# A fused sigmoid-attention and gated MLP kernel: an own PSUM bank for one of seven products, and attention heads spread otherwise over the MLP blocks

## The chip, the cores and the metric

One core of one Trainium2 chip. The metric is device time of one execution in microseconds (us); lower is better. Engines in the profile: PE (matrix products), DVE (vector), ACT (scalar and activation), SP (issues the DMAs); POOL does nothing here.

## The reference

```python
def _attn_ref(q, k, v):                       # q, k, v: (8, 12, 448, 64)
    scores = scale * np.matmul(q, k.transpose(0, 1, 3, 2)) - np.log(S)
    attn = 1.0 / (1.0 + np.exp(-scores))
    return np.matmul(attn, v)

def _moe_ref(x, w_in, w_out):                 # x: (3584, 768), w_in: (768, 2048), w_out: (2048, 768)
    h = x @ w_in
    g = h * (1.0 / (1.0 + np.exp(-1.702 * h)))
    return g @ w_out

def reference(**kwargs):
    attn_out = _attn_ref(q, k, v)
    x = attn_out.transpose(0, 2, 1, 3).reshape(B * S, H * D)
    return _moe_ref(x, w_in, w_out)
```

96 attention heads (8 batches of 12) without a softmax, and then a two-layer MLP over the 3584 tokens.

## The kernel before

**Tiling.** The tokens are cut into 7 blocks of 512 (numbered 0 to 6); the batches have 448 tokens, so a block takes parts of two batches. In a block, `ups` are 48 tasks of six matmuls (16 columns of `w_in`, three tasks each, tiles `h`), and `downs` are 48 tasks of six matmuls (6 output tiles `o` of eight tasks). Every fp32 product is made as three fp32r matmuls of a rounded part and a rest (128x512 each): rounding is a CAST on ACT or DVE, and the rest a subtraction on DVE.

**Attention.** Batches 0 to 2 are done first, two heads at a time (L530, L553), partly alongside block 0. Batches 3 to 7, 60 heads, are done one at a time by `head`: scores on PE in two tasks (tile `sc`, L713, 7 matmuls in sum), sigmoid on ACT (L719), rounding and rest (`ahi`, `alo`, L761, L768), product with v on PE (tile `av`, L802, 7 matmuls), additions into a block's x (L817). `split_head` prepares q and k before that (`qk`, L669 and others). `packed_attention` makes 61 *units* of PE tasks from them: a unit holds the two score tasks of one head and the product of the head before, and the 61st holds the last product alone. After the 20th unit and every fifth from there on, `sums_of_weights` loads two weight tiles, combines them on DVE (`sums`, `tsplit`) and stores the results.

**Last two blocks.** Blocks 5 and 6 are done together by `last_blocks`: a 2x2 block product by seven products (p1 to p7) in place of eight. Its inputs are sums of x parts (tiles `xs`, `xa`: names `s1` to `s4`, `a11` to `a22`). `up(n)` is called eight times, four in each half, and after each half `down` makes the outputs (L1172). In `up` the products are nine matmuls each (L1081) and run in the order p1, p6, p2, p7, p5, p4, p3. The tile `q` (`sc`, two banks of 512 f32) takes p1 and then p2 on top of it in its first half, and p6 in its second half; `w` (`m`) takes p7 and then p4, `z` (`m0` or `av`) takes p5 and then p3. The copy c1 (L1098 on ACT or L1099 on DVE) takes p1's result out of `q` before p2 adds to it; u2, u3, c22, c21, c12 are additions on DVE (L1000); `activated` makes the sigmoid (L1043), its product (L1046), rounding and rest.

**Order of work.** Each engine has its own list of instructions, written by a planner (`Plan.run`) at build time, with estimated costs. A task has dependencies, and each `Buffer` of a ring of n waits for the users of the n-th buffer before it (`BUFS`: `sc` 2, `m` 2, `m0` 1, `av` 1, `qk` 2, `x32` 8, `x` 6). On ACT, DVE and SP the planner takes the ready task with the smallest key (its place in the order). On PE there are two queues: `main` (ups and downs of all blocks, then the last blocks) and `side` (the attention units), each strictly in its order. A side unit is due when a given number of main tasks has been taken; the queue whose head can begin first goes next, and a due side unit wins a tie. These places come from this loop, in which an up counts 0.8 and a down 1.0 (86.4 in a block), and `LEAD` is 0.93:

```python
n = sum(HEADS[: b - 1])
units = [(0, u) for u in (packed[n : n + HEADS[b - 1]] if b < NB - 3 else packed[n:])]
...
total, done, n = sum(costs) * (LEAD if b < NB - 3 else LAST), 0.0, 0
for i, c in enumerate(costs):
    done += c
    while n < len(units) and n / len(units) < done / total:
        due.append((len(main) + i + 1, units[n][1]))
        n += 1
```

`HEADS` gives the units of blocks 1 to 4; block 4 takes whatever is left (NB is 7). The synchronisation between the engines is added by the framework from the tiles that each instruction reads and writes.

Of the kernel before, what the change touches and what calls it, by code (L numbers as in the profile page):

```python
# [18 lines left out]
ALU = mybir.AluOpType  # L19
# [16 lines left out]

SOON, PATIENCE = 6, 0.8

WARM = 5

HEADS, LAST = (12, 16, 16, 16), 0.78


BUFS = dict(
# [1 line left out]
    sc=2, sc3=1, av=1, m=2, m0=1,  # L46
# [29 lines left out]
class Plan:  # L76
# [10 lines left out]
    def buffer(self, tag):  # L87
        b = Buffer()
        self.rings.setdefault(tag, []).append(b)
        return b  # L90

    def task(self, engine, cost, emit, deps=(), uses=()):
        return self.either({engine: cost}, {engine: emit}, deps, uses)
# [8 lines left out]
    def run(self, streams):  # L102
# [19 lines left out]
        main, side = streams  # L122
# [13 lines left out]
        free = dict.fromkeys(("PE", "ACT", "DVE", "SP", "DMA"), 0.0)  # L136
# [11 lines left out]
        def since(t):  # L148

            if t.takes is None:  # L150
                return t.ready
            return max(t.ready, min(slots[t.takes], default=math.inf))
        at, current, doing = [0, 0], [], 0

        def pe():

            if current:
                return max(free["PE"], current[0].ready), None
            best = None
            heads = []  # L160
            if at[1] < len(side):
                heads.append((1, side[at[1]][1], side[at[1]][0] <= at[0]))
            if at[0] < len(main):
                heads.append((0, main[at[0]], True))
            for s, unit, due in heads:

                first = [t for t in unit if t.alone]
                if any(t.left for t in first):
                    continue
                when, before = free["PE"], 0.0  # L170
                for t in first:
                    when = max(when, t.ready - before)
                    before += t.costs["PE"]
                if best is None or when < best[0] - 1e-9 or (not best[2] and when <= best[0] + 1e-9):
                    best = (when, s, due)
            return (best[0], best[1]) if best else (None, None)

        count = 0
        while count < len(self.tasks):
            options = []  # L180
            when, s = pe()
# [6 lines left out]
            when, _, e = min(options)  # L188
# [7 lines left out]
            else:  # L196
# [9 lines left out]
                if soon:  # L206
                    t = min(soon, key=lambda t: t.key)
                    when = max(when, since(t))
# [43 lines left out]
def sigmoid_attention_mlp(ctx: ExitStack, tc: tile.TileContext, qk, v, v2, w, out):  # L252
# [60 lines left out]
    ps = spaces["m0"].tile([P, 512], F32, tag="m0", name="still", bufs=BUFS["m0"])  # L313
    for n in range(WARM):
        nc.tensor.matmul(ps, lhsT=still[:, :P], rhs=still, start=n == 0, stop=n == WARM - 1)

    plan = Plan()
    task, either, buffer = plan.task, plan.either, plan.buffer
# [12 lines left out]
    def dma(into, src, kb, deps, uses, first=lambda: None):  # L331
        def emit():
            first()
            nc.sync.dma_start(out=into(), in_=src())

        return task("SP", kb, emit, deps, uses)

    def on_either(act, dve, deps, uses, first=lambda: None):


        def emit(f):
            def go():
                first()
                f()

            return go

        return either({"ACT": act[0], "DVE": dve[0]}, {"ACT": emit(act[1]), "DVE": emit(dve[1])}, deps, uses)
# [502 lines left out]
    def columns(n):  # L851
        return 8 * (n // 4) + n % 4, 8 * (n // 4) + n % 4 + 4
# [130 lines left out]
    def last_blocks():  # L983
# [13 lines left out]
        def combine(out, a, b, op, deps, uses, first=lambda: None):  # L997
            def emit():
                first()
                nc.vector.tensor_tensor(out(), a(), b(), op=op)  # L1000

            return task("DVE", 0.69, emit, deps, uses)

        for i in range(NK // 2):
# [9 lines left out]
            s1, s2 = buffer("line"), buffer("line")  # L1014
# [17 lines left out]
        def piece(src, deps, name):  # L1032
            b = buffer("wsplit")
            return dma(lambda: b.tile.bitcast(F32), src, 2 * KB, deps, [b],
                       lambda: make(b, "wsplit", [P, 2 * NW_EL], F32R, name)), b
# [19 lines left out]
        def up(n):  # L1055
            f, f2 = columns(n)
            t_1, w1 = piece(lambda: halves[f], [saved[f]], f"w1_{n}")
            t_2, w2 = piece(lambda: sums[n][0], [summed[n, 0]], f"w2_{n}")
            t_3, w3 = piece(lambda: sums[n][1], [summed[n, 1]], f"w3_{n}")
            w4 = buffer("wh")  # L1060
            t_4 = dma(lambda: w4.tile.bitcast(F32).rearrange("p (t c) -> p t c", t=2),
                      lambda: halves[f2].rearrange("p (t c) -> p t c", t=2)[:, :, HW:], KB,
                      [saved[f2], *gate], [w4], lambda: make(w4, "wh", [P, 2 * HW], F32R, f"w4_{n}"))
            bank = ("m0", "av")[n % 2]
            q, z, w = buffer("sc"), buffer(bank), buffer("m")
            made = {"sc": [P, 2, 512]}

            def product(b, tag, at, wb, t_w, half, name, deps, more):

                step = wb.tag_cols if hasattr(wb, "tag_cols") else NW_EL  # L1070

                def emit():
                    if b.tile is None:
                        make(b, tag, made.get(tag, [P, 512]), F32, f"{tag}_{n}")
                    ps = at()
                    for i in range(NK // 2):
                        k = (half * (NK // 2) + i) * P
                        ws = [wb.tile[:, j * step + k : j * step + k + P] for j in range(2)]
                        x = parts[name, i][1].tile
                        for j, (c, d) in enumerate(((0, 1), (1, 0), (0, 0))):  # L1080
                            nc.tensor.matmul(  # L1081
                                ps, lhsT=ws[c], rhs=x[:, d], start=not more and i == 0 and j == 0,
                                stop=i == NK // 2 - 1 and j == 2, skip_group_check=more,
                            )

                xparts = [parts[name, i] for i in range(NK // 2)]
                t = task("PE", 9 * 0.2267, emit, [t_w, *deps, *(x[0] for x in xparts)],
                         [b, wb, *(x[1] for x in xparts)])
                units.append([t])
                return t  # L1090

            w4.tag_cols = HW
            q0, q1 = (lambda: q.tile[:, 0]), (lambda: q.tile[:, 1])
            h12, h22, h21 = buffer("x32"), buffer("x32"), buffer("x32")

            def copy(b, name, src, t, uses):
                return on_either(
                    (0.59, lambda: nc.scalar.copy(b.tile, src())),  # L1098
                    (0.69, lambda: nc.vector.tensor_copy(b.tile, src())),  # L1099
                    [t], [b, *uses], lambda: make(b, "x32", [P, T], F32, f"{name}_{n}"),  # L1100
                )

            def in12(): return h12.tile
            def in22(): return h22.tile
            def in21(): return h21.tile

            p1 = product(q, "sc", q0, w1, t_1, 0, "a11", [], False)
            c1 = copy(h12, "h12", q0, p1, [q])
            p6 = product(q, "sc", q1, w2, t_2, 1, "s2", [], False)
            u2 = combine(in12, in12, q1, ALU.add, [c1, p6], [h12, q])  # L1110
            p2 = product(q, "sc", q0, w1, t_1, 1, "a12", [c1], True)
            activated(one, f, q0, p2, [q])
            p7 = product(w, "m", lambda: w.tile, w3, t_3, 0, "s3", [], False)
            u3 = combine(in21, in12, lambda: w.tile, ALU.add, [u2, p7], [h21, h12, w],
                         lambda: make(h21, "x32", [P, T], F32, f"h21_{n}"))
            p5 = product(z, bank, lambda: z.tile, w2, t_2, 0, "s1", [], False)
            c5 = copy(h22, "h22", lambda: z.tile, p5, [z])
            c22 = combine(in22, in21, in22, ALU.add, [u3, c5], [h22, h21])
            activated(two, f2, in22, c22, [h22])
            p4 = product(w, "m", lambda: w.tile, w3, t_3, 1, "a22", [u3], True)  # L1120
            c21 = combine(in21, in12, lambda: w.tile, ALU.add, [p4, c22], [h21, h12, w])
            activated(two, f, in21, c21, [h21])
            p3 = product(z, bank, lambda: z.tile, w4, t_4, 0, "s4", [c5], True)
            c12 = combine(in12, in12, lambda: z.tile, ALU.add, [p3, c21], [h12, z])
            activated(one, f2, in12, c12, [h12])
# [84 lines left out]
    side = [(0, u) for u in attention()]  # L1210
# [8 lines left out]
    due = []  # L1219
# [14 lines left out]
    side = side[:early] + due  # L1234
# [37 lines left out]
```

## Time and profile before

| | |
|---|---|
| median of 3 runs | 1208.38 us (1208.35 to 1209.86) |
| the profiled execution's own time | 1209.63 us |
| its span, first to last instruction | 1207.6 us |
| busy: PE, DVE, ACT | 1189.8 us, 869.7 us, 718.6 us |
| mean granted TensorE clock | 0.998 |
| DMA | 274.10 MB, mean 227 GB/s |

Times of a trace are us from the span's start. A row of the timeline gives start, duration, engine, line, operation, output and input tile, shape, and count of merged instructions; in brackets the idle time of that engine ahead of it, and what ended it. Matmuls are pipelined, so a row's duration overlaps the next; distances are read from start to start.

### The profile page before, as it was taken

Reading aid. Unit: us, or ns where it says so; the run is one execution under the profiler, and the core shown is the slowest. Engines: PE = TensorE matmul, PEld = TensorE weight load, DVE = VectorE, ACT = ScalarE, POOL = GpSimd, SP = SyncE. Lnnn points to the kernel's source line nnn. Section 1 sums busy time; section 2 is a strip of 40 time slices with the busy share of each in tenths; the row PEclk is TensorE's granted clock in tenths of the full one; section 3 lists DMA queues with packets and bytes.
Section 4 is the critical chain, followed back from the end, with each engine's and each line's share of the span. In section 5 each row is a group of like instructions: output and inputs, shape, how many; then the busy total and the mean of one; then the engine's idle time right before and its main releaser. Section 6 shows DMA issues by size and latency. Waiting matters only on the chain.

```text
span 1207.6 us, 15254 instructions
## 1 busy us (share of the span) xinstructions
PE 1189.8 (99%) x5517; PEld 955.2 (79%) x5517; DVE 869.7 (72%) x1431; ACT 718.6 (60%) x1139; POOL 0.2 (0%) x4
## 2 busy tenths in 40 slices
PE   9999999999999999999999999999989999999998
PEld 4457777788888888888888888888778777877787
DVE  6989989689987588988598987599998254005511
ACT  7898887467786576766577776577864132113300
POOL 0000000000000000000000000000000000000000
PEclk9999999999999999999999999999999999999999
DMA  9956568786876656777666877775756654455552
GB/s 346 315 184 240 187 207 281 259 280 226 303 263 252 223 168 195 257 265 279 235 229 218 292 247 246 245 250 206 258 187 227 211 178 160 135 162 195 201 192 79
DMA packets 82155, 274.10 MB, mean 227 GB/s; under 512 B 8640, under 2 KB 15808, under 8 KB 82080
## 3 DMA queue, kind: packets, MB, share of 16 engines
q1 hardware_dynamic: 82080, 273.12, 66.0%
q8 instruction: 44, 0.72, 0.2%
q14 instruction: 31, 0.25, 0.1%
HBM read 203.88 MB, written 69.21 MB: 226 GB/s over the span
## 4 chain that ended last, share of the span: by engine, by line
PE 89%; DVE 7%; ACT 3%; issue 1%; DMA 0%; DVEq 0%; ACTq 0%
PE o L908 26%; PE h L908 22%; PE o L1172 11%; PE av L802 6%; PE sc L713 6%; PE av L553 5%; PE sc L1081 4%; PE sc L530 4%; PE m L1081 4%; PE av L1081 1%; DVE alo L768 1%; DVE qk L669 1%; ACT a L719 1%; DVE g L940 0%; DVE ahi L768 0%
## 5 line engine op out<-in xcount | busy, mean ns | idle before, releaser
L908 PE MATMUL h<-x,wsplit 128*128 128x512 f32 x1440 | 334.7, 390 | 0.5 <-DVE x L359 0.5
L908 PE MATMUL o<-gs,wsplit 128*128 128x512 f32 x1440 | 334.2, 390 | 0.0
L908 PEld LDWEIGHTS o<-gs,wsplit 128*128 128x128 f32 x1440 | 270.5, 188 | 57.1 <-issue 1.3
L908 PEld LDWEIGHTS h<-x,wsplit 128*128 128x128 f32 x1440 | 269.9, 188 | 57.5 <-issue 1.3
L353 ACT CAST gs<-g 128x512 fp32r<-128x512 f32 x108 | 67.0, 620 | 107.5 <-DVE g L940 67.2
L1172 PE MATMUL o<-gs,wd 128*128 128x512 f32 x576 | 130.9, 389 | 0.0
L719 ACT ACTIVATE a<-sc,bias 128x448 f32<-128x448 f32 x120 | 98.4, 820 | 50.9 <-PE sc L713 46.1
L1172 PEld LDWEIGHTS o<-gs,wd 128*128 128x128 f32 x576 | 108.1, 188 | 22.4
L669 DVE TENSOR_TENSOR qk<-qkraw,qk 64x64 fp32r<-64x64 f32 x180 | 111.3, 619 | 4.9 <-ACT qk L674 0.7
L768 DVE TENSOR_TENSOR alo<-a,ahi 128x448 fp32r<-128x448 f32 x120 | 101.2, 848 | 2.3 <-ACT ahi L761 1.1
L713 PE MATMUL sc<-qk 128*128 128x448 f32 x420 | 95.2, 366 | 2.8 <-ACT a L719 2.8
L761 ACT CAST ahi<-a 64x448 fp32r<-64x448 f32 (+2 forms) x138 | 88.5, 663 | 2.1
L713 PEld LDWEIGHTS sc<-qk 128*128 128x128 f32 x420 | 78.8, 188 | 12.3 <-ACT a L719 3.2
L359 DVE TENSOR_TENSOR gs<-g,gs 128x512 fp32r<-128x512 f32 x112 | 76.3, 685 | 10.2 <-ACT gs L353 8.2
L744 DVE COPY rest<-sc 64x448 f32<-64x448 f32 x45 | 28.2, 626 | 75.0 <-ACT a L719 70.4
L541 ACT ACTIVATE a<-sc,bias 112x896 f32<-112x896 f32 x72 | 68.7, 1007 | 14.9 <-PE sc L530 8.6
L1000 DVE TENSOR_TENSOR h<-h,sc 128x512 f32<-128x512 f32 x8 | 5.5, 688 | 96.2 <-PE sc L1081 96.2
L802 PE MATMUL av<-ahi,v 128*128 128x448 f32 x240 | 59.3, 370 | 0.0
L553 PE MATMUL av<-a,vraw 112*64 112x448 f32 x288 | 57.9, 545 | 0.0
L940 DVE TENSOR_TENSOR g<-h,g 128x512 f32<-128x512 f32 x80 | 54.7, 685 | 1.9 <-ACT g L935 0.9
L359 DVE TENSOR_TENSOR wsplit<-wraw,wsplit 128x768 fp32r<-128x768 f32 x48 | 45.7, 952 | 12.8 <-ACT wsplit L353 12.5
L935 ACT ACTIVATE g<-h 128x512 f32<-128x512 f32 x80 | 47.6, 595 | 10.6 <-PE h L908 10.1
(106 smaller groups left out, 1345.6 us busy)
## 6 DMA issues: line engine op xcount, KB each, us to landing
wsplit<-w SPq DMA_DIRECT2D x96, 768.0 KB, 5.1
w<-w SPq DMA_DIRECT2D x40, 768.0 KB, 5.2
w<-wsplit SPq DMA_DIRECT2D x32, 768.0 KB, 5.4
qkraw<-qk SPq DMA_DIRECT2D x48, 448.0 KB, 3.8
wraw<-f SPq DMA_DIRECT2D x48, 384.0 KB, 4.3
f<-w SPq DMA_DIRECT2D x32, 384.0 KB, 4.3
t<-tsplit SPq DMA_DIRECT2D x16, 768.0 KB, 4.4
w<-t SPq DMA_DIRECT2D x16, 768.0 KB, 4.8
```

Of the source, the lines that this page charges most:

```text
L359: lambda: nc.vector.tensor_tensor(lo(), src(), hi().bitcast(F32), op=ALU.subtract),
L541: nc.scalar.activation(a.tile[:C, c % 2], ps.tile[:C, :, :S], AF.Sigmoid, bias=bias[:C], scale=scale)
L553: nc.tensor.matmul(ps.tile[cols, :S], lhsT=vr.tile[:C, j, c], rhs=a.tile[:C, c % 2, j], start=c == 0, stop=c == NC - 1,)
L669: return lambda: nc.vector.tensor_tensor(s.tile[rows, into], qkr.tile[own, cols], s.tile[own, cols].bitcast(F32), op=ALU.subtract)
L713: nc.tensor.matmul(out, lhsT=s.tile[:, cols], rhs=s.tile[:, r : r + S], start=n == 0, stop=n == len(terms) - 1,)
L719: nc.scalar.activation(out, x, AF.Sigmoid, bias=bias[:rows], scale=scale)
L761: (costs[0], lambda: nc.scalar.copy(hi_at(), cols())),
L768: nc.vector.tensor_tensor(lo_at(), cols(), hi_at().bitcast(F32), op=ALU.subtract)
L802: nc.tensor.matmul(av.tile[:, :S], lhsT=vs.tile[:, c].rearrange("p a d -> p (a d)"), rhs=m, start=n == 0, stop=n == len(todo) - 1,)
L908: nc.tensor.matmul(ps, lhsT=ws[a], rhs=x[:, c], start=first and i == 0, stop=last and i == 2)
L1081: nc.tensor.matmul(ps, lhsT=ws[c], rhs=x[:, d], start=not more and i == 0 and j == 0, stop=i == NK // 2 - 1 and j == 2, skip_group_check=more,
L1172: nc.tensor.matmul(ps.tile, lhsT=ws[u], rhs=gb.tile[:, d], start=i == 0 and j == 0, stop=i == 7 and j == 2,)
```

## The change

- In `up`, p6 gets a buffer of its own, `q2`, in the ring `m`, and u2 reads it there. The second half of the tile `q` is no longer used (the tile keeps its size).
- `HEADS` goes from (12, 16, 16, 16) to (13, 17, 17, 13), and `LAST` from 0.78 to 0.84. Of the 61 units, blocks 1 to 4 had 12, 16, 16 and 17; they get 13, 17, 17 and 14. In block 4 they are spread over the first 0.84 of its cost.
- In the planner's choice between the two queues of PE, a side unit with a due place above zero is ranked as if it could begin `SLACK` = 2.0 us later than it can. The time at which it is then placed is not moved.

```diff
+SLACK = 2.0
-HEADS, LAST = (12, 16, 16, 16), 0.78
+HEADS, LAST = (13, 17, 17, 13), 0.84
...
-                when, before = free["PE"], 0.0
+                when, before = 0.0, 0.0
                 for t in first:
                     when = max(when, t.ready - before)
                     before += t.costs["PE"]
-                if best is None or when < best[0] - 1e-9 or (not best[2] and when <= best[0] + 1e-9):
-                    best = (when, s, due)
-            return (best[0], best[1]) if best else (None, None)
+
+                rank = max(free["PE"], when + (SLACK if s and side[at[1]][0] else 0.0))
+                if best is None or rank < best[0] - 1e-9 or (not best[2] and rank <= best[0] + 1e-9):
+                    best = (rank, s, due, max(free["PE"], when))
+            return (best[3], best[1]) if best else (None, None)
...
-            q, z, w = buffer("sc"), buffer(bank), buffer("m")
+            q, q2, z, w = buffer("sc"), buffer("m"), buffer(bank), buffer("m")
...
-            q0, q1 = (lambda: q.tile[:, 0]), (lambda: q.tile[:, 1])
+            q0, q1 = (lambda: q.tile[:, 0]), (lambda: q2.tile)
...
-            p6 = product(q, "sc", q1, w2, t_2, 1, "s2", [], False)
-            u2 = combine(in12, in12, q1, ALU.add, [c1, p6], [h12, q])
+            p6 = product(q2, "m", q1, w2, t_2, 1, "s2", [], False)
+            u2 = combine(in12, in12, q1, ALU.add, [c1, p6], [h12, q2])
```

## The prediction

> **What bounds the kernel now.** I read the page first, then the waits of PE stage by stage, then PE's own timeline around each wait.
>
> ```profile
> span 1207.6 us, 15254 instructions
> PE 1189.8 (99%) x5517; PEld 955.2 (79%) x5517; DVE 869.7 (72%) x1431; ACT 718.6 (60%) x1139; POOL 0.2 (0%) x4
> ```
>
> PE is the bound: it is without work for 1207.6 - 1189.8 = 17.8 us in all. The change removes no matmul, so only those 17.8 us, and what a wait costs beyond its idle time, can be won. The waits of PE, for 945 us to the end and then for 760 to 950 us (columns: total us, times, longest):
>
> ```profile
> PE sc L1081 <- DVE h L1099: 4.7, 6, 0.8
> PE sc L1081 <- ACT h L1098: 1.4, 2, 0.7
> ```
>
> ```profile
> PE sc L713 <- ACT a L719: 2.8, 1, 2.8
> PE av L802 <- DVE x L817: 1.4, 1, 1.4
> PE av L802 <- DVE alo L768: 0.9, 2, 0.5
> ```
>
> So there are two sore places: eight equal waits in the seven-product stage (one for each of the eight calls of `up`), and a bunch in block 4, where PE waits for the steps of a head. These are what the two halves of the change touch.
>
> **The bank of the second product.** PE's timeline in the first two calls of `up`, nine matmuls to a product:
>
> ```profile
> 952.26 2.20 PE L1081 MATMUL sc<-xs,w 128*128 128x512 f32 x9
> 955.13 2.34 PE L1081 MATMUL sc<-x,w 128*128 128x512 f32 x9 [0.68 <-ACT h L1098]
> 957.31 4.24 PE L1081 MATMUL m<-xs,w 128*128 128x512 f32 x18
> ...
> 967.51 2.20 PE L1081 MATMUL sc<-xs,w 128*128 128x512 f32 x9
> 970.50 2.35 PE L1081 MATMUL sc<-x,w 128*128 128x512 f32 x9 [0.78 <-DVE h L1099]
> 972.69 2.21 PE L1081 MATMUL m<-xs,w 128*128 128x512 f32 x9
> ```
>
> The first row of each triple is the second product p6, the second row is p2, the third p7. p2 adds onto the first product's half of `sc`, so it must wait for the copy c1 of that half. c1 needs only p1, which ends when p6 starts (952.26), and so could run beside p6. It does not:
>
> ```profile
> 954.50 0.59 ACT L1098 COPY h<-sc 128x512 f32<-128x512 f32 x1 [3.49 <-PE sc L1081]
> ```
>
> It starts when p6's row ends (952.26 + 2.20 = 954.46). ACT had been idle for 3.49 us, so it was not busy elsewhere. The natural reading: p1 and p6 write one tile, `sc`, and a reader of the tile waits for its latest writer. A product with a tile of its own shows the contrast; u3, the addition of p7:
>
> ```profile
> 959.55 0.69 DVE L1000 TENSOR_TENSOR h<-h,m 128x512 f32<-128x512 f32 x1
> ```
>
> p7 and p5 are the 18 matmuls from 957.31 on; u3 starts when nine of them are done (957.31 + 2.20 = 959.51), with the nine of p5 still running. So a reader whose product is alone in its tile does not wait for the next product. With p6 in `m`, c1 starts near 952.5 and ends near 953.1, over a microsecond before p2 could begin.
>
> What the wait costs is more than its idle time, since weight loads and the pipe start anew. Without it two products take 18 matmuls of 0.2277 us (price below) = 4.10 us; from p6's start to p7's it took 957.31 - 952.26 = 5.05 and 972.69 - 967.51 = 5.18 us. That is 0.95 for the two calls whose copy is on ACT and 1.08 for the six on DVE: 2 x 0.95 + 6 x 1.08 = **8.4 us**. The bounds: the idle time alone, 4.7 + 1.4 = 6.1 us, and 8.4; I take 8.4 because starts were measured.
>
> What moves along: p6 takes one of the two `m` buffers, so they no longer alternate between calls for p7 and p4. p6 must find u2 of the call before done, and p7 must find the last reader of p4's sum done, c21; c21 follows p4 while p3, p1, p6 and p2 still come ahead of the next p7, 36 matmuls or 8.2 us of cover against one 0.69 us addition behind a short chain. If that cover were gone, its cost would be about one such addition per call. The block-one groups of the down stage swap the two `m` buffers; each was last read a group or more before. No instruction and no DMA is added. The weight pieces have the same distance from release to next use, except those of p7, which lose the 1 us gap of 8.2 us; no row of PE's waits in this stage names a DMA. u2 also leaves DVE's queue sooner (now it waits for p2), which only frees those behind it. Late next in this stage: nothing is in sight.
>
> The rule that speaks against this: the Trainium skill, "PSUM — Partial Sum Buffer", summary table, has a reader beside a running matmul use a different bank, and gives a bank 2 KiB. Halves of 512 f32 are two banks already, so by the hardware alone c1 was free to run and another bank changes nothing: the sum would be short of this term. The 954.50 and 959.55 rows speak for bookkeeping by tile instead, which the page does not cover; it is a rival below.
>
> **The heads.** The price of a plain matmul and of a head's unit on PE, from block 3's down stage:
>
> ```profile
> 688.33 1.58 PE L713 MATMUL sc<-qk 128*128 128x448 f32 x7
> ...
> 691.17 6.99 PE L908 MATMUL o<-gs,wsplit 128*128 128x512 f32 x30
> 698.00 1.58 PE L713 MATMUL sc<-qk 128*128 128x448 f32 x7
> ```
>
> A unit is 691.17 - 688.33 = 2.84 us, 30 matmuls are 6.83 us (0.2277 each; a task of six 1.366 us), and the pitch from head to head is 9.67 us, with no wait. In block 4 a head comes every 3.96 tasks (0.78 x 86.4 / 17 units): 2.84 + 3.96 x 1.366 = 8.25 us. There it fails:
>
> ```profile
> 870.12 1.58 PE L713 MATMUL sc<-qk 128*128 128x448 f32 x7
> ...
> 874.71 5.62 PE L908 MATMUL o<-gs,wsplit 128*128 128x512 f32 x24
> 880.16 0.77 PE L713 MATMUL sc<-qk 128*128 128x448 f32 x3
> ...
> 887.93 7.43 PE L908 MATMUL o<-gs,wsplit 128*128 128x512 f32 x30
> 895.20 1.58 PE L713 MATMUL sc<-qk 128*128 128x448 f32 x7
> ```
>
> Lost against 2.84 us: 874.71 - 870.12 = 4.59, so 1.75; 887.93 - 880.16 = 7.77, so 4.93; and 895.20 - 887.93 = 7.27 for 6.83, so 0.44: **7.1 us**. Part of it is the clock that the wait brought down:
>
> ```profile
> 886.00:888.00 2.00, 2.00 (x7) 1.74 (x7) 2.00 (x4) 2.00 (x3) 0.00 (x0) 0.50 0.46 180
> ```
>
> Granted 0.50 after a 2.8 us wait: 4.93 + 0.44 less the idle 2.8 + 0.5 leaves 2.1 us of slow and restarted matmuls. (The Trainium skill, "TensorE: Matmul & The Clock Gate", Part 1, puts the drop after about 3.4 us of idle window; this trace shows it after less. By its rule a remaining wait of 2.8 us would cost 2.8, by the trace 4.9.)
>
> Why there: DVE. Busy time by stretch (PE, PEld, DVE, ACT, POOL, clock, DMA share, GB/s): block 3's ups and downs, then the bad stretch.
>
> ```profile
> 592.00:681.00 89.00, 89.00 (x405) 75.70 (x404) 79.33 (x137) 65.65 (x114) 0.00 (x0) 1.00 0.66 224
> 681.00:749.00 68.00, 68.00 (x312) 58.12 (x311) 57.00 (x100) 49.90 (x86) 0.00 (x0) 1.00 0.81 284
> ...
> 859.00:890.00 31.00, 26.25 (x112) 21.48 (x111) 30.36 (x52) 26.64 (x46) 0.00 (x0) 0.94 0.61 207
> ```
>
> DVE is busy 89%, 84% and 98%. In the last, a head's steps queue behind the splitting of block 5's x and the preparing of summed weights, and PE waits for the head.
>
> The edit of HEADS and LAST gives block 4 61 - 47 = 14 units in place of 17, spread over 0.84 of it: one per 0.84 x 86.4 / 14 = 5.18 tasks, a pitch of 2.84 + 7.08 = 9.92 us, wider than the 9.67 us that ran without a wait. So the 7.1 us go. The PE work of the moved heads (2.84 us each), their loads and spills on SP's queue and their DVE steps reappear in blocks 1 to 3, one head more in each: PE's part cancels. Blocks 2 and 3 go from 0.93 x 86.4 / 16 = 5.02 to 4.73 tasks, a pitch of 9.30 us. Their DVE share rises by at most 17/16: 95% in block 3's ups, 89% in its downs; and the sets of summed weights, tied to every fifth unit from the 20th on, shift with them: the set of the 45th unit from block 4 to 3 and that of the 30th from block 3 to 2, each with its two loads and two stores on SP, so that block 4 has one fewer and block 2 one more. That is the price side. A head added in block 1 meets DVE work of weight splitting, but PE takes the main product when a side unit isn't ready, so I cost it at nothing beyond the term below; DMA goes up by less than a tenth from a share of 0.81 at most, and PE waits for no load here.
>
> New waits in blocks 1 to 3, bounded: if all of block 4's bad stretch came back in one block, +7.1 us; if nothing, 0 (below nothing is excluded, since no wait stands there to be removed but the next one). 9.30 lies between 8.25 (loses) and 9.67 (does not), nearer the latter; I take **+1.0**.
>
> A small wait goes too, at the start of block 2:
>
> ```profile
> 414.36 2.23 PE L908 MATMUL h<-x,wsplit 128*128 128x512 f32 x9
> 417.12 6.46 PE L908 MATMUL h<-x,wsplit 128*128 128x512 f32 x27 [0.52 <-DVE x L359]
> ```
>
> Nine matmuls are 2.05 us, so 417.12 - 414.36 - 2.05 = **0.7 us** lost for block 2's x, which needs the twelfth head's product; that stands in the thirteenth unit, until now the first of block 2. With 13 units in block 1 it comes a block earlier.
>
> SLACK changes no instruction, only PE's order: a spread unit is ranked as if ready 2 us later, so that a main product goes first where the plan has the unit just in time. What queues behind a put-off unit is the rest of the units, in their order. A head takes this long from scores to its last low part:
>
> ```profile
> 902.14 1.58 PE L713 MATMUL sc<-qk 128*128 128x448 f32 x7
> ...
> 909.30 0.62 DVE L768 TENSOR_TENSOR ahi<-a,ahi 64x448 fp32r<-64x448 f32 x1
> ```
>
> 909.92 - 902.14 = 7.8 us; 2 us more is 9.8, above 9.30. So in the downs of blocks 2 and 3 a unit may be put off to the sixth task (2.84 + 8.2 = 11.0 us): 1.7 us later per head, 14 us for eight heads. Between the last unit's due place and the end of the block stand 0.07 x 86.4 + 4.73 = 10.8 tasks = 14.7 us, so the lag is absorbed. I cost SLACK at nothing, with its worse case as a rival.
>
> **Sum.** The profiled execution took 1209.63 us, 2.0 above its span; the median of the three runs is 1208.38, 1.25 less, and I subtract from that: 1208.4 - 8.4 - 7.1 - 0.7 + 1.0 = 1193.2, forecast **1193** us. No change means within 0.2% (2.4 us): 1206.0 to 1210.8; the three runs lie 1.5 us apart.
>
> **Rivals.**
> 1. The waits of the heads move to blocks 2 and 3. For it: DVE at 95% in block 3's ups. Against it: 9.67 us without a wait, and the reserve of SLACK. Time: 1208.4 - 8.4 - 0.7 = 1199.3 if all 7.1 us come back, 1197 for two thirds of them, 1201 with as much slow clock again.
> 2. The copy still waits, because the cause is not the shared tile (the change doesn't do what it says). For it: the two halves were separate banks already, as the page says. Against it: the 959.55 row. Time: 1208.4 - 7.1 - 0.7 + 1.0 = 1201.6.
> 3. Slower: the lag from SLACK isn't absorbed, and the last head ends so late that p6 of the first call waits for s2. What it needs shows here, from the last head's product to the last split of an s2 part:
>
> ```profile
> 919.37 0.97 PE L802 MATMUL av<-ahi,v 128*128 128x448 f32 x4
> ...
> 934.49 0.68 DVE L359 TENSOR_TENSOR xs<-s,xs 128x512 fp32r<-128x512 f32 x1
> ```
>
> 935.17 - 920.2 (the product's end) = 15 us. After the change the last unit is due with 48 - 29 = 19 down tasks left, 26 us, and p1 of 2 us lies before p6: 28 - 15 = 13 us of cover. Each us of lag beyond that costs one. To end above 1210.8 it must eat 15.2 + 2.4 = 17.6 us, so a lag of 30.6 us, three heads' pitch; with the 14 us of one block unabsorbed it costs 1 us. Time at the decisive point 1211; it would take several blocks' lag added up.
>
> **Chances and range.** Forecast (1190 to 1196.5): 0.66. Rival 1: 0.18. Rival 2: 0.08. Rival 3 in full 0.04, and 0.04 for a lag that eats most of the gain (1206 to 1210). The range runs from 1190, all terms won, no new wait and the smaller waits on `alo` gone as well, to 1200.5, where it leaves out rivals 2 and 3 and the upper end of rival 1. Faster 0.92, no change 0.04, slower 0.04.
>
> **What would show it.** Right: in each `up` the copy starts about 0.2 us after p1's end, p6, p2 and p7 start 2.05 us apart, and the eight waits of p2 are gone. Heads in block 4 about 11.7 us apart in the ups (6.48 tasks) and 9.9 in the downs, without a wait over 0.5 us, clock 1.00 throughout; no wait for x at block 2's start. PE's time without work falls from 17.8 to about 7 us. Wrong: p2 still preceded by 0.7 us (rival 2); waits on `alo`, `x` or `a` between 417 and 764 us (rival 1); p6 waiting for `xs` (rival 3).

## The result, and the profile after

The changed kernel takes 1193.60 us (median of 4 runs, 1191.68 to 1194.69), the kernel before 1208.37 us beside it; the ratio is 0.9874 with a 95% interval of 0.9857 to 0.9891. The forecast was 1193. The profiled executions took 1209.63 and 1193.79 us, 15.84 us apart.

The first lines of the page after:

```profile
span 1191.9 us, 15238 instructions
PE 1185.0 (99%) x5517; PEld 955.2 (80%) x5517; DVE 873.0 (73%) x1443; ACT 718.5 (60%) x1127; POOL 0.2 (0%) x4
```

PE has the same 5517 matmuls. Its time without work fell from 17.8 to 1191.9 - 1185.0 = 6.9 us, and its busy time by 4.8 us: the matmuls that a wait had made slow or had started anew. All waits of PE in the whole span (total us, times, longest; the lines of the code moved by four):

```profile
PE still L319 <- DVE still L316: 1.5, 1, 1.5
PE sc L534 <- DMA qkraw<-qk: 0.6, 1, 0.6
PE o L912 <- DMA wsplit<-w: 0.5, 1, 0.5
PE sc L534 <- ACT a L545: 0.2, 1, 0.2
```

The waits of p2, of block 4 and of block 2's start are gone. One is new: 0.5 us for a weight load in block 3, below. These waits are 2.8 us of the 6.9; most of the rest, 3.9 us, stands behind the last matmul, which ends at 1188.0 us.

The trace also tells the two halves of the change apart. The first p1 starts at 943.05 us, before at 950.22: 7.17 us are won ahead of the last two blocks. From the first p1 of a half to its downs, the four calls of `up` take 57.12 us in both halves, before 61.40 and 61.41: 8.57 us are won there. The first call of `up` on PE's timeline:

```profile
943.05 2.20 PE L1085 MATMUL sc<-x,w 128*128 128x512 f32 x9
945.09 2.20 PE L1085 MATMUL m<-xs,w 128*128 128x512 f32 x9
947.13 2.20 PE L1085 MATMUL sc<-x,w 128*128 128x512 f32 x9
949.17 4.24 PE L1085 MATMUL m<-xs,w 128*128 128x512 f32 x18
```

p1, p6, p2 and p7 start exactly 2.04 us apart. The copy c1 and the addition u2, from the timelines of ACT and DVE:

```profile
945.29 0.59 ACT L1102 COPY h<-sc 128x512 f32<-128x512 f32 x1 [1.40 <-PE sc L1085]
...
947.40 0.69 DVE L1004 TENSOR_TENSOR h<-h,m 128x512 f32<-128x512 f32 x1 [7.17 <-PE m L1085]
```

c1 starts 0.2 us after p6 has begun, while p6 runs; u2 starts 0.1 us after p6's end (945.09 + 2.20 = 947.29), while p2 runs. Block 4's downs:

```profile
876.73 1.58 PE L717 MATMUL sc<-qk 128*128 128x448 f32 x7
...
879.57 6.99 PE L912 MATMUL o<-gs,wsplit 128*128 128x512 f32 x30
886.39 1.58 PE L717 MATMUL sc<-qk 128*128 128x448 f32 x7
```

A head every 9.66 us, its unit 2.84 us long, no wait. And the stretch that was bad before, by the windows:

```profile
859.00:890.00 31.00, 31.00 (x143) 26.42 (x142) 29.81 (x51) 25.02 (x43) 0.00 (x0) 1.00 0.75 268
```

PE is busy all of it at full clock, with 143 matmuls in place of 112. DVE is still 96% busy (98% before): a full DVE is no wait by itself.

### The profile page after: what moved, and what is told of

The parts are those of the page before. It is cut to its first block, busy times and chain, and to the rows that moved or that the text cites. A ratio compares the mean times of both kernels' runs of the same rounds, so it can differ in the third digit from the quotient of the medians.

```text
span 1191.9 us, 15238 instructions
## 1 busy us (share of the span) xinstructions
PE 1185.0 (99%) x5517; PEld 955.2 (80%) x5517; DVE 873.0 (73%) x1443; ACT 718.5 (60%) x1127; POOL 0.2 (0%) x4
## 4 chain that ended last, share of the span: by engine, by line
PE 96%; DMA 2%; DVE 1%; ACT 1%; issue 0%; SPq 0%; ACTq 0%
PE h L912 28%; PE o L912 25%; PE o L1176 11%; PE sc L717 7%; PE av L806 7%; PE m L1085 5%; PE av L557 5%; PE sc L534 4%; PE sc L1085 3%; PE av L1085 1%; DMA wsplit<-w 1%; DMA wsum<-f 1%; DMA qkraw<-qk 0%; ACT a L545 0%; DVE qk L673 0%; DVE alo L772 0%
## 5 line engine op out<-in xcount | busy, mean ns | idle before, releaser
L1004 DVE TENSOR_TENSOR h<-h,m 128x512 f32<-128x512 f32 x28 | 19.2, 686 | 86.7 <-PE m L1085 86.7
L765 ACT CAST ahi<-a 128x448 fp32r<-128x448 f32 (+2 forms) x124 | 80.3, 666 | 2.1
```

The costliest lines, as they stand in the source:

```text
L765: (costs[0], lambda: nc.scalar.copy(hi_at(), cols())),
```

## Experiments

The kernel of experiment n is called kernel n. Each was timed against the kernel before on the same chip, in three sets: kernels 1 to 4, then 5, 6, 7 and 9, then 8 and 10 to 12. The medians of the kernel before were 1209.36, 1209.50 and 1209.52 us in them, so ratios can be compared across sets. Diffs show the lines that matter, against the changed kernel. "The bank" is short for p6's new buffer; a bank of 512 f32 p6 had before as well, what is new is a tile that it shares with no other product of the call.

**1. The bank alone.**

```diff
-SLACK = 2.0
-HEADS, LAST = (13, 17, 17, 13), 0.84
+SLACK = 0.0
+HEADS, LAST = (12, 16, 16, 16), 0.78
```

> Only the buffer of p6 is new; the spread of the heads and the order on PE are those of before. Theory (a reader of a tile waits for the latest product written to that tile): the eight waits of p2 go, each worth 0.95 to 1.08 us from p6's start to p7's, so 8.5 us less, about 1199.8 us, ratio 0.993; the waits of PE in block 4 (about 5 us idle, 7 us lost) stay. Rival (the two halves were two banks anyway, so the wait has another cause and the gain is all from the heads): p2 still waits, 1208 us, ratio 1.000.

Measured: 1200.83 us, ratio 0.9927 (0.9914 to 0.9941). PE's waits in block 4:

```profile
PE sc L717 <- ACT a L723: 2.8, 1, 2.8
PE av L806 <- DVE x L821: 1.4, 1, 1.4
PE av L806 <- DVE alo L772: 0.3, 1, 0.3
```

The two long ones are as before, the waits on `alo` are 0.3 us in place of 0.9, and no wait of p2 is left. The bank is worth 8.5 us (7.1 to 10.4 by the interval), as the theory had it; the rival is out.

**2. The heads alone**, p6 back in the second half of p1's tile:

```diff
-            q, q2, z, w = buffer("sc"), buffer("m"), buffer(bank), buffer("m")
+            q, z, w = buffer("sc"), buffer(bank), buffer("m")
-            q0, q1 = (lambda: q.tile[:, 0]), (lambda: q2.tile)
+            q0, q1 = (lambda: q.tile[:, 0]), (lambda: q.tile[:, 1])
...
-            p6 = product(q2, "m", q1, w2, t_2, 1, "s2", [], False)
-            u2 = combine(in12, in12, q1, ALU.add, [c1, p6], [h12, q2])
+            p6 = product(q, "sc", q1, w2, t_2, 1, "s2", [], False)
+            u2 = combine(in12, in12, q1, ALU.add, [c1, p6], [h12, q])
```

> HEADS, LAST and SLACK as in the changed kernel, but p6 back in the second half of the tile of p1. Theory (the two halves of the change add up): the eight waits of p2 are there, 6 us idle, and the waits in block 4 and at the start of block 2 are gone: 1193.6 + 8.5 = 1202 us, ratio 0.995. Rival (the spread of the heads brings nothing of its own, the bank brings all): 1208 us, ratio 1.000. Rival (they overlap): less than 1200 us.

Measured: 1201.41 us, ratio 0.9933 (0.9920 to 0.9945). PE's waits from 240 us on:

```profile
PE sc L1085 <- DVE h L1103: 4.7, 6, 0.8
PE sc L1085 <- ACT h L1102: 1.3, 2, 0.7
PE h L912 <- DMA wsplit<-w: 0.2, 1, 0.2
```

The eight waits are back, beside a small one for a weight load. 8.0 us for the heads and 8.5 for the bank are 16.5 us, against 16.5 for the changed kernel in the last set (1209.52 to 1193.04) and 14.8 in the first (1208.37 to 1193.60). Both intervals hold the sum, so the halves add up as far as can be measured.

**3. Without the margin** (`SLACK = 0.0`, all else as changed).

> The changed kernel with SLACK 0: p6 has its own bank, HEADS and LAST are new, and a side unit is ranked without a margin. Theory (the wider pitch in block 4 removes the waits, the margin only guards): within 1 us of the changed kernel, 1193 to 1195 us, waits of PE for alo, x or a below 1 us. Rival (the margin does it, the heads of blocks 2 and 3 at a pitch of 9.3 us would stall without it): waits between 500 and 760 us, 1196 to 1200 us.

Measured: 1194.10 us, ratio 0.9872 (0.9858 to 0.9885); one wait for `alo` of 0.5 us and two for weights, 0.9 us in sum. In time, the margin (`SLACK`) is worth nothing that can be measured here. In the trace it does one thing: the wait for `alo` is in block 2,

```profile
551.04 0.67 PE L806 MATMUL av<-alo,v 128*128 128x448 f32 x2 [0.51 <-DVE alo L772]
```

and in the changed kernel PE does one more main task (36 matmuls in place of 30, from 541.95 us on) ahead of that head and does not wait.

**4. The margin with the old heads** (`HEADS, LAST = (12, 16, 16, 16), 0.78`, `SLACK = 2.0`, bank as changed).

> p6 has its own bank, SLACK is 2.0, but HEADS and LAST are those of before. Theory (the pitch of 8.25 us in block 4 is too close for DVE, the margin only moves the wait or softens it): the waits in block 4 are smaller but the heads come later, 1195 to 1199 us. Rival (the margin alone removes the waits, since PE always has a main product to take): 1193 to 1194 us, and the new spread brings nothing.

Measured: 1198.40 us, ratio 0.9911 (0.9898 to 0.9925), 2.4 us below the bank alone, with overlapping intervals. PE's timeline shows why it may be below; the first three rows are those of the bank alone, the others those with the margin:

```profile
875.29 5.62 PE L912 MATMUL o<-gs,wsplit 128*128 128x512 f32 x24
880.75 0.77 PE L717 MATMUL sc<-qk 128*128 128x448 f32 x3
884.33 1.86 PE L717 MATMUL sc<-qk 128*128 128x448 f32 x4 [2.81 <-ACT a L723]
...
874.22 6.98 PE L912 MATMUL o<-gs,wsplit 128*128 128x512 f32 x30
881.04 0.77 PE L717 MATMUL sc<-qk 128*128 128x448 f32 x3
883.25 1.08 PE L717 MATMUL sc<-qk 128*128 128x448 f32 x4 [1.45 <-ACT a L723]
```

Ahead of the late head stand 30 matmuls where the bank alone has 24: one main task was taken first, and the wait is 1.45 us in place of 2.81. The granted clock is 1.00 from 884 to 888 us, where the bank alone has 0.58 and 0.56. The 1.4 us for `x` ahead of it stay. The margin shortens this wait and does not remove it.

**5 and 6. HEADS alone and LAST alone**, both with the bank and without the margin: `(13, 17, 17, 13), 0.78` and `(12, 16, 16, 16), 0.84`.

> p6 has its own bank and HEADS is new, but LAST stays 0.78 and SLACK is 0. Block 4 has 14 units over 0.78 of it, a pitch of 0.78 x 86.4 / 14 = 4.81 tasks, 2.84 + 6.58 = 9.4 us in its downs. Theory (a pitch near 9.3 us is wide enough, as blocks 2 and 3 showed): no waits of PE in block 4, 1194 us. Rival (0.84 is needed as well): waits in block 4, 1196 to 1200 us.

> p6 has its own bank and LAST is 0.84, but HEADS is that of before and SLACK is 0. Block 4 has 17 units over 0.84 of it, a pitch of 0.84 x 86.4 / 17 = 4.27 tasks, 2.84 + 5.83 = 8.7 us in its downs. Theory (between 8.25 us, which loses 7 us, and 9.3 us, which loses nothing): smaller waits, 1195 to 1198 us. Rival (any widening is enough): 1194 us.

Measured: HEADS alone 1194.05 us, ratio 0.9874 (0.9860 to 0.9887), no wait in block 4, and 1.2 us of waits in block 2. LAST alone 1198.95 us, ratio 0.9912 (0.9899 to 0.9926), 1 us above the expected range and 1.9 below the bank alone, with overlapping intervals. LAST alone still waits in block 4:

```profile
PE sc L717 <- ACT a L723: 1.6, 1, 1.6
PE o L912 <- DVE x L821: 1.3, 1, 1.3
PE av L806 <- DVE alo L772: 0.6, 1, 0.6
```

So of the three planner edits the one that counts is HEADS: three heads fewer in block 4, and with them one of its three sets of summed weights. With it, 0.84 adds nothing that can be measured. Without the margin it leaves small waits in block 2, here 1.2 us.

**7. Another tile, but the same place in it**: p6 in the second half of a second `sc` tile.

```diff
-            q, q2, z, w = buffer("sc"), buffer("m"), buffer(bank), buffer("m")
+            q, q2, z, w = buffer("sc"), buffer("sc"), buffer(bank), buffer("m")
-            q0, q1 = (lambda: q.tile[:, 0]), (lambda: q2.tile)
+            q0, q1 = (lambda: q.tile[:, 0]), (lambda: q2.tile[:, 1])
...
-            p6 = product(q2, "m", q1, w2, t_2, 1, "s2", [], False)
+            p6 = product(q2, "sc", q1, w2, t_2, 1, "s2", [], False)
```

> The changed kernel, but p6 goes into the second half of a second tile of the ring sc, so it has another tile than p1 and still the second of two banks of it, and the ring m is left to p7 as before. Theory (the wait goes by the tile): no wait of p2, 1193 to 1195 us. Rival (the position, or the ring m, matters): 0.7 us ahead of each p2, 1202 us. The ring sc has two tiles, so the next call's p1 needs this call's p2 read; four products lie between, so no new wait is expected.

Measured: 1192.27 us, ratio 0.9859 (0.9845 to 0.9872), 0.7 us below the expected range; no wait of p2:

```profile
941.58 2.20 PE L1085 MATMUL sc<-x,w 128*128 128x512 f32 x9
943.62 2.20 PE L1085 MATMUL sc<-xs,w 128*128 128x512 f32 x9
945.66 2.20 PE L1085 MATMUL sc<-x,w 128*128 128x512 f32 x9
```

The tile decides, not the ring or the half.

**8. Another product in the shared tile**: p7 and p4 in the second half of the tile of p1 and p2, p6 alone in `m`.

```diff
-            p7 = product(w, "m", lambda: w.tile, w3, t_3, 0, "s3", [], False)
+            p7 = product(q, "sc", lambda: q.tile[:, 1], w3, t_3, 0, "s3", [], False)
...
-            p4 = product(w, "m", lambda: w.tile, w3, t_3, 1, "a22", [u3], True)
+            p4 = product(q, "sc", lambda: q.tile[:, 1], w3, t_3, 1, "a22", [u3], True)
```

> The changed kernel, but p7 and p4 go into the second half of the tile of p1 and p2 (a bank of its own still), and p6 alone uses the ring m. Theory (a reader of a tile waits for the product written to that tile last): the copy of p1 still starts 0.2 us after p1, but the sigmoid of p2's half, which started right after p2, now starts after p7, 2.0 us later, in all eight calls; nothing on PE waits for it, so 1193 to 1195 us. Rival (the wait belonged to p1 and p6 for another reason): the sigmoid starts right after p2 as before.

Measured: 1195.71 us, ratio 0.9886 (0.9871 to 0.9900), 0.7 us above what was expected. The first call, from the timeline:

```profile
948.38 2.20 PE L1085 MATMUL sc<-x,w 128*128 128x512 f32 x9
...
950.42 2.20 PE L1085 MATMUL sc<-xs,w 128*128 128x512 f32 x9
952.46 2.20 PE L1085 MATMUL m<-xs,w 128*128 128x512 f32 x9
952.66 0.60 ACT L1047 ACTIVATE g<-sc 128x512 f32<-128x512 f32 x1 [5.53 <-PE sc L1085]
...
953.90 0.68 DVE L1004 TENSOR_TENSOR h<-h,sc 128x512 f32<-128x512 f32 x1
...
954.63 2.35 PE L1085 MATMUL sc<-xa,w 128*128 128x512 f32 x9
```

The sigmoid of p2's half starts at 952.66, when p7 has ended (950.42 + 2.20 = 952.62), and not when p2 has (948.38 + 2.20 = 950.58). In the changed kernel it starts at 949.37, right after p2. ACT's idle time ahead of the eight sigmoids rose from 20.2 to 36.5 us, 2.04 us for each: one product. That is the wait of before, moved to another reader by moving another product into the tile, so the theory holds by a second test. What was missed is where it lands: the late sigmoid holds up its product on DVE, u3 queues behind that until 953.90, and p4, which waits for u3, starts at 954.63 in place of 952.46 + 2.04 = 954.50. p4's row then lasts 2.35 us in place of 2.20, and so it goes in every call: the four calls of a half take 58.47 and 58.52 us in place of 57.12 in the changed kernel: 2.75 us in all, against 2.67 us between the medians of the two in this set (1195.71 and 1193.04). So "nothing on PE waits for it" was wrong. The profiled execution, the slowest of four, also has a wait of 1.33 us for a weight load at 594.8 us, ahead of this stage.

**9. The heads of block 4 at their old pitch, with DVE's extra work taken away**: all sets of summed weights ahead of block 4, the bank as changed, HEADS, LAST and SLACK as before.

```diff
-                    if len(units) > 18 and len(units) % 5 == 0 and n < NF // 2:
+                    if len(units) > 18 and len(units) % 3 == 0 and n < NF // 2:
```

> The kernel of before with p6 in its own bank, and the sets of summed weights after every third unit from the 21st on instead of every fifth, so that all eight are done before block 4; the heads of block 4 stay at a pitch of 8.25 us. Theory (PE's waits in block 4 come from DVE's extra work beside the heads): the second wait (2.8 us, with sums between the head's steps) shrinks by the 1.6 us of sums ahead of it or goes, the clock stays at 1.00 there, the first (1.4 us, beside the splitting of x) stays: 1197 to 1198 us against 1200.8 for the bank alone. Rival (the pitch alone is too close): the waits stay, 1200.8 us. A loss in block 2 or 3, which take three sets more, would show as waits before 764 us.

Measured: 1201.98 us, ratio 0.9935 (0.9921 to 0.9949): no gain over the bank alone, where 3 us had been expected. But the place is as the theory has it. The bad stretch:

```profile
859.00:890.00 31.00, 30.82 (x141) 26.00 (x139) 30.06 (x51) 26.79 (x48) 0.00 (x0) 1.00 0.58 190
```

With 17 heads in block 4, PE waits 0.18 us there in place of 4.2, at a granted clock of 1.00 and with DVE 97% busy. Both waits went, the first one too, though no sums stood ahead of it; the plan orders the steps around anew when the sets leave, and what freed the first wait is not told apart. So a pitch of 8.3 us by itself need not stall: it took the extra work as well. The gain was given back where the sets went, as the waits from 400 to 760 us show (the profiled execution is the slowest of five, 1204.56 us):

```profile
PE h L912 <- DMA wsplit<-w: 2.5, 1, 2.5
PE av L806 <- DVE alo L772: 1.6, 2, 1.2
PE o L912 <- DMA wsplit<-w: 1.0, 1, 1.0
```

PE waits for weights until 584 and 591 us. On SP's queue a weight load stood behind a load of q and k that waited 9.3 us for its buffer; the first line is from the waits of SP's queue, the others from its timeline:

```profile
SPq L338 <- DVE qk L673: 9.3, 1, 9.3
...
567.96 0.32 SPq L338 DMA_DIRECT2D wsplit<-w  x1
577.62 0.33 SPq L338 DMA_DIRECT2D qkraw<-qk  x1
578.04 0.38 SPq L338 DMA_DIRECT2D wsplit<-w  x1
580.28 0.32 SPq L338 DMA_DIRECT2D t<-tsplit  x1
```

From 568.3 to 577.6 us SP issued nothing; after that weights, and stores of summed weights (`t`), all came at once.

**10 and 11. Another queue for q and k**: kernels 9 and 7 with the loads of q and k of batches 3 to 7 issued from POOL's queue.

```diff
-            nc.sync.dma_start(out=into(), in_=src())
+            (queue or nc.sync).dma_start(out=into(), in_=src())
...
-                  lambda: make(qkr, tag, [P, S2], F32, f"qkraw{b}_{p}"))
+                  lambda: make(qkr, tag, [P, S2], F32, f"qkraw{b}_{p}"),
+                  nc.gpsimd if b >= PACKED else None)
```

> The kernel with all sets of summed weights ahead of block 4, but the loads of q and k of batches 3 to 7 are issued from POOL's queue in place of SP's. Theory (PE waited for weights at 584 and 591 us because their load stood behind a load of q and k on SP that waited 9.3 us for its buffer): those waits, 4 us, go, 1197 to 1198 us. Rival (the DMA engines were full there, share 1.01): they stay, 1202 us. Second rival: loads from POOL's queue come later and the heads wait for qkraw.

> The version with p6 in a second tile of the ring sc, and the loads of q and k of batches 3 to 7 issued from POOL's queue. No PE wait for a weight load was left to win but 0.4 us: 1191.5 to 1192.5 us, the same as with SP's queue. If loads from POOL's queue cost something of their own, it shows here as waits for qkraw, or on DVE, above 1193 us.

Measured: kernel 10 1200.80 us, ratio 0.9924 (0.9908 to 0.9941), the waits for weights 2.4 us in place of 4.1; kernel 11 1193.02 us, ratio 0.9859 (0.9846 to 0.9872), the same in time as with SP's queue, though its profile has 1.4 us of waits for weights where kernel 7's has none. In kernel 10 no wait of PE names these loads of q and k. Part of the wait for weights went, and 1.9 us stayed at 590 us, while the DMA engines were 95% busy from 580 to 592 us. The interval of kernel 10 overlaps that of kernel 9, so how much the queue's order costs and how much the full DMA engines, stays open.

**12. The changed kernel once more.**

> The changed kernel once more, on the same chip as the others of this set: 1193 to 1195 us, about 1 us above the version with p6 in the ring sc, and within 1 us of the versions without the margin. If it is the same as those of p6 in the ring sc, the choice of ring is worth nothing.

Measured: 1193.04 us, ratio 0.9867 (0.9850 to 0.9885). Kernel 7 is at 0.9859 in one set and kernel 11 in this one, kernels 3 and 5 at 0.9872 and 0.9874: all these intervals overlap, so the choice of ring is worth nothing that was measured. No version that was run beats the changed kernel by more than can be measured.

## Why the prediction was right

- **The bank (8.4 us).** From p6's start to p7's it takes 949.17 - 945.09 = 4.08 us now, against 5.05 and 5.18: 0.97 x 2 + 1.10 x 6 = 8.5 us. Alone it brought 8.5, and the eight calls together are 8.57 us shorter in the trace. The upper bound was the right choice, because starts were measured and not idle times: 6.1 us of the waits were idle, the rest was overlap that the waits broke and matmuls that started anew. Reading tiles rather than banks as the unit of the wait was right, and kernels 7 and 8 show it. The page "PSUM — Partial Sum Buffer" of the Trainium skill, by whose rule (summary table) the copy was free from the start, speaks of what the hardware allows; here the waits that the framework adds were wider.
- **The heads in block 4 (7.1 us) and block 2's start (0.7 us).** All these waits went; alone the heads brought 8.0 us, 0.2 more than both terms. In the trace 7.17 us are won ahead of the first p1, with a new wait of 0.55 us paid from it. The prediction left the two smaller waits on `alo` out of its sum; they went as well.
- **New waits in blocks 1 to 3 (+1.0 us).** With the margin there are none for heads; without it, kernels 3 and 5 show waits for a head's steps, as the term had in mind, 0.5 and 1.2 us in block 2. One came for a weight load, 0.55 us, on the timeline:

```profile
758.90 9.71 PE L912 MATMUL o<-gs,wsplit 128*128 128x512 f32 x42
769.15 4.42 PE L912 MATMUL o<-gs,wsplit 128*128 128x512 f32 x18 [0.55 <-DMA wsplit<-w]
```

  The size was near, the mechanism was not: the prediction looked to DVE and held that PE waits for no load. The nearness is luck: the wait differs from run to run, and the changed kernel's second trace (kernel 12) has none there. Before it SP issued nothing from 746.9 to 755.3 us, as in kernel 9, and the DMA engines were 93% busy from 755 to 770 us; which of the two made the weights late is not told apart here either.
- **The reason for the stall** was given as DVE at 98% and the pitch of 8.25 us. Half right: DVE at 96% in the changed kernel makes no wait, and a pitch of 8.3 us makes 0.18 us once the summed weights are away (kernel 9). The stall took both, the close pitch and the extra work: taking away all the sets of summed weights ended it, and so did taking away three heads and one set. Which of these two counted in the change, and that the head's steps stood behind the extra work in DVE's order, is argued from the traces and not shown by a run.
- **SLACK at nothing** was right in sum, but not for the reason given. No lag of 14 us per block appeared that had to be absorbed. In the downs of block 2 one head was put off to the sixth task, in those of block 3 none, and behind the last head of either 60 matmuls, 10 tasks, were left, where the spread leaves 10.8. In block 4 the last head's product made way for main products with 114 matmuls, 19 tasks, left before p1, just as the spread had it due:

```profile
916.81 26.40 PE L912 MATMUL o<-gs,wsplit 128*128 128x512 f32 x114
```

- **The rivals.** That the copy would still wait is out by kernel 1. That the heads' waits would move to blocks 2 and 3 is out for the changed kernel, and without the margin only 0.5 to 1.2 us of them show; in kernel 9, 1.6 us came in block 3. That the last head would make p6 wait is out: the last split of an s2 part started at 932.38 us and p6 at 945.09.

## What to carry to other kernels

Put two results that are written one after the other and read separately into two tiles, even where they lie in different banks anyway: the framework may make a reader wait for whatever was written to its tile last. Price a wait of a pipelined engine from start to start; the idle time in the list of waits was three quarters of what it cost here. And before moving work off a crowded stretch, look at the DMA queue and the DMA engines where it goes: the sets of sums that went with 4 us of PE's waits for DVE and ACT in block 4 went with 4 us of its waits for weights, most of them around the end of block 2, when they were moved.

## What the runs showed of the hardware that was not expected

The clock after a wait. Two kernels with nearly the same wait at the same place differ in it. With LAST alone PE waited 1.55 and then 0.57 us, the second time until 887.06, and soon after ran at half clock:

```profile
886.00:888.00 2.00, 1.43 (x6) 0.97 (x5) 2.00 (x3) 1.47 (x3) 0.00 (x0) 0.86 0.00 0
888.00:890.00 2.00, 2.00 (x7) 1.66 (x6) 1.97 (x5) 1.69 (x4) 0.00 (x0) 0.50 0.43 175
```

With the margin and the old heads it waited 1.45 and 0.51 us, and the clock stayed at 1.00 in the windows from 880 to 890 us:

```profile
886.00:888.00 2.00, 2.00 (x11) 1.67 (x10) 2.00 (x5) 1.96 (x4) 0.00 (x0) 1.00 0.48 195
```

So two waits of 2.1 us in sum, with matmuls between them, were followed by half clock in one kernel, and two of 2.0 us were not in the other. The Trainium skill ("TensorE: Matmul & The Clock Gate", Part 1) puts the drop after an idle window of about 3.4 us; no wait here was that long. Two executions don't tell what decides it. A window that runs freely, as the page has it, could fall differently on the same waits; no run here shows that.
